# Sinkhorn normalisation moved onto 128 partitions as two chains, with half-size first loads and a new issue order

## The chip, the core and the metric

The kernel runs on one core of a Trainium2 chip. A core has five engines that run their own instruction streams: TensorE (PE in the profile; its weight loads are shown apart as PEld), VectorE (DVE), ScalarE (ACT), GpSimd (POOL) and SyncE (SP, which here only issues DMAs). They meet through semaphores. PSUM is the memory that TensorE writes and that DVE and ACT read; SBUF is the working memory.

The metric is the device time of one execution in microseconds, median of the runs. Before the change it is 155.96 us (three runs, 155.92 to 155.98).

## The reference

The computation is a block-sorted attention followed by a gated MLP, for 4 batches, 8 heads, 768 tokens, head size 64. Each head has an 8x8 matrix `sort_net`, normalised in five Sinkhorn rounds. Its result mixes the eight 96-token blocks of k and v, and each block of q attends only to its own mixed block.

```python
P = sort_net                                     # (4, 8, 8, 8)
for _ in range(5):
    P = np.exp(P - np.max(P, axis=-1, keepdims=True))
    P = P / (np.sum(P, axis=-1, keepdims=True) + 1e-09)
    P = P / (np.sum(P, axis=-2, keepdims=True) + 1e-09)
k_sorted = np.einsum('bhij,bhjcd->bhicd', P, k_b)      # v_sorted likewise
...                                              # per block: softmax(q k^T / 8) v
x = attn_out.transpose(0, 2, 1, 3).reshape(B, S, H * D)
h = np.maximum(x @ w_in, 0.0)                    # 512 -> 1024, halves u and v
v_n = (v - mu) / np.sqrt(var + 1e-06)
v_s = np.einsum('ts,bsd->btd', w_spatial, v_n) + b_spatial[None, :, None]
return (u * v_s) @ w_out
```

## The kernel before

The whole program is written as a list of short items, `ORDER`. Each item names a function (`u_KT`, `u_SC`, ...) and its arguments, and the items are issued in exactly that order; every engine takes its own instructions from the list in sequence. No scheduler changes it. The first argument of an item that uses TensorE is one of four PSUM buffers (0 to 3); an item that wants a buffer waits until the previous user's result has been copied out. The letter A or D says whether ACT or DVE makes that copy.

The items that matter here, with the engine work of each:

- `S0`, `SK:n`: load `sort_net` as 32 partitions (batch and head) by 64 values, then one Sinkhorn round n: an exponential on ACT, then six short DVE instructions (row sums, reciprocal, product, column sums, reciprocal, product; lines 238 to 249). Round 4 ends with a transpose on DVE (line 251).
- `MC`, `PR`: eight bf16 products that spread the normalised matrices over 128 partitions (line 256). `P0:lo:hi` multiplies them by a mask into `pd(0)`, the mixing matrices of batch 0, on DVE (line 270). `PC` copies the spread matrices to SBUF, and `PD:b:lo:hi` makes the mixing matrices of heads lo to hi of batch b from that copy on GpSimd (line 282).
- `L:what:b:lo:hi`: a load with cast from fp32 to bf16, issued on GpSimd's DMA queue (line 171 for q, k, v); `LH` loads half of q of batch 0 as fp32 on SP's queue and `QC` casts it on ACT. Loads rotate through eight buffers and eight semaphores.
- `KT`, `VT`: twelve products of two heads of k or v with `pd` (line 383) and one copy. `QT`, `QQ`: transposes of q (line 314). `VB`, or `VM` and `VC` (a copy and DMAs), bring mixed v into the layout that attention wants.
- `SC`: eight score products (line 442) and the exponential on ACT (line 447). `AT`: eight products with mixed v (line 488), a reciprocal and a product on DVE (lines 495, 496). `XT`, `XX` or `XD`: transposes of the attention output, on TensorE or by DMA.
- `VP`, `UP` (the two halves of the first linear layer, lines 554 and 597), `ST`, `LN`, `LA` (layer normalisation), `SP` (token mixing, line 609), `GT` (gate), `OP`, `OE`, `OS` (last layer, copy, store). The items from `SH` on are the end of the last batch, in smaller pieces.
- `DM:ps:n:w`: n products of zeros, w columns wide (line 226), whose results nobody reads.

The order around the change: DVE prepares constants, the five rounds `SK:0` to `SK:4` follow, with `DM` items and two `QT` items between them on TensorE; `PR`, four `P0` items and `PC` end the preparation, and the first `VT` and `KT` follow. The loads are issued in the order v, k, second half of q of batch 0, then v, q, k of batch 1, the weights, and so on.

An alternative path (`general_path`) repeats the computation with maxima subtracted. It is taken only when a check of the sums (`CK`, `CF`, `LF`) fires, which it does not with these inputs.

Of the kernel before, what the change touches and what calls it, by code (L numbers as in the profile page):

```python
# [21 lines left out]
KT:0:D:0:2 SC:2:0:0:1 VB:3:D:0:0 PD:1:4:8 KT:1:A:0:1 QT:0:D:0:2 IV:1 QT:2:A:0:3 VB:3:D:0:1 SC:0:0:1:0 VT:1:D:0:3  # L22
VT:2:A:0:2 L:wsa L:q:2:0:8 SC:3:0:0:0 PD:3:0:4 PD:3:4:8 BI AT:0:0:0:1 L:k:2:0:8 VB:1:D:0:3 SC:2:0:1:1 AT:3:0:0:0
VM:0:A:1:0 VB:1:D:0:2 SC:2:0:2:0 AT:3:0:1:0 SC:0:0:3:0 AT:1:0:2:0 SC:2:0:2:1 AT:3:0:1:1 VM:0:A:1:2 AT:2:0:3:0
XT:1:A:0:0:0 VM:0:D:1:3 QQ:3:D:1:2 SC:1:0:3:1 VM:2:D:1:1 XT:0:A:0:1:0 KT:1:A:1:2 L:q:3:0:8 AT:3:0:3:1 VC:1:4:8
KT:0:A:1:1 AT:2:0:2:1 KT:1:A:1:0 VC:1:0:4 QQ:3:D:1:0 KT:0:A:1:3 PD:2:0:4 XT:2:D:0:0:2 XT:1:D:0:1:2 PD:2:4:8 L:wo
SC:3:1:0:1 SC:0:1:2:0 VP:2:D:0:0:1 ST:0:0 SC:0:1:1:1 SC:1:1:3:1 ST:0:1 VP:3:A:0:4:5 VP:2:A:0:2 VP:1:A:0:3 ST:0:5
L:v:3:0:8 WW:2:A:4 ST:0:3 SC:3:1:3:0 AT:0:1:0:1 UP:1:A:0:1:0 ST:0:2 ST:0:4 AT:0:1:3:1 UP:2:A:0:0:0 LN:0:0:6 AT:3:1:2:0
# [37 lines left out]
def kernel(  # L66
# [123 lines left out]
    def load_sort_net():  # L190
        queue("S").dma_start(out=p_all, in_=sort_net.rearrange("b h i j -> (b h) i j"))
# [635 lines left out]
```

## Time and profile before

| | |
|---|---|
| median of three runs | 155.96 us |
| profiled execution, span from first to last instruction | 154.5 us (1.5 us less than the median of the runs) |
| PE busy, share of the span | 146.7 us, 95% |
| DVE busy | 115.4 us, 75% |
| ACT busy | 85.5 us, 55% |
| GpSimd busy | 39.4 us, 25% |
| mean granted TensorE clock | 0.999 of full speed |
| loads through GpSimd's queue | 12.19 MB, 48.8% of the time of the 16 DMA engines |

The profile is one execution, taken by the hardware profiler. Its views are read as follows. A group row gives line, engine, operation, output <- input and shape, number of instructions, busy time and mean duration in ns, then the idle time ahead of them and what ended it. A timeline row gives start, duration, engine, line, operation. A piece of the chain (start, duration, what) belongs to the one path that, followed back from the last instruction, released every next step. A row of windows gives a stretch, then busy time and number of instructions on PE, PEld, DVE, ACT and POOL, then granted clock, DMA share and GB/s. A busy PE is not a PE at its peak, since its instructions are pipelined.

### The profile page before, as it was taken

The page shows a single profiled execution, that of the slowest core. Times are in us where ns is not written, and L with a number is a line of the kernel's source. Part 1 is how long each engine was busy: PE and PEld are TensorE (multiplying, and loading weights), DVE is VectorE, ACT ScalarE, POOL GpSimd, SP SyncE. Part 2 cuts the span into 40 slices and gives each one's busy share as a digit, 9 for nine tenths or more (in the row PEclk, how much of TensorE's full clock was granted, in tenths as well). Part 3 has the DMA queues.
Part 4 walks back from the last instruction along what each step waited for, and adds up shares of the span by engine and source line. Part 5 has one row for each costly group of instructions (what it writes and reads, how often), then busy time and mean ns, then how long its engine had stood idle before and what let it go on. Part 6 is the DMA issues. An engine that isn't in the chain of part 4 may idle for free.

```text
span 154.5 us, 4033 instructions
## 1 busy us (share of the span) xinstructions
PE 146.7 (95%) x1689; PEld 95.7 (62%) x1689; DVE 115.4 (75%) x258; ACT 85.5 (55%) x116; POOL 39.4 (25%) x45
## 2 busy tenths in 40 slices
PE   6988988999999999999999999999999999999991
PEld 2436866764667777456777654656876556774760
DVE  3787889968899976299974886697977629855742
ACT  3345989787979245997777057357650072260040
POOL 7953663292020007000000044000000406103630
PEclk9999999999999999999999999999999999999999
DMA  2999999999999999990069358704708400307756
GB/s 68 270 204 203 204 206 204 209 216 248 223 205 256 205 231 245 208 195 15 4 118 125 67 102 167 182 3 37 205 0 215 163 0 4 132 4 284 268 191 220
DMA packets 30693, 24.36 MB, mean 158 GB/s; under 512 B 10384, under 2 KB 27792, under 8 KB 30672
## 3 DMA queue, kind: packets, MB, share of 16 engines
q0 software_dynamic: 14432, 12.19, 48.8%
q1 hardware_dynamic: 15664, 11.23, 28.8%
q10 hardware_dynamic: 576, 0.66, 1.2%
q8 instruction: 14, 0.23, 0.6%
q14 instruction: 7, 0.06, 0.1%
HBM read 24.78 MB, written 6.29 MB: 201 GB/s over the span
## 4 chain that ended last, share of the span: by engine, by line
PE 84%; DMA 7%; ACT 2%; DVE 2%; POOL 1%; issue 1%; POOLq 0%; ACTq 0%
PE ps L609 15%; PE ps L554 14%; PE ps L597 14%; PE ps L635 10%; DMA k_in<-in_k_dram 7%; PE ps L442 5%; PE ps L488 5%; PE ps L665 5%; PE ps L383 4%; PE ps L685 3%; PE ps L314 2%; PE ps L410 2%; PE ps L518 2%; ACT ex_all L447 2%; PE ps L531 1%; PE ps L401 1%
## 5 line engine op out<-in xcount | busy, mean ns | idle before, releaser
L626 POOL TENSOR_TENSOR gt<-z,u_sb 128x768 bf16<-128x768 f32 x7 | 11.4, 1640 | 77.0 <-DVE z L615 47.6
L447 ACT ACTIVATE ex_all<-ps 96x768 bf16<-96x768 f32 x32 | 24.7, 806 | 5.7 <-PE ps L442 5.5
L609 PE MATMUL ps<-wspT,v_sb 128*128 128x384 bf16 x144 | 25.1, 326 | 0.0
L597 PE MATMUL ps<-xT,w_in_sb 128*128 128x384 bf16 x128 | 22.8, 326 | 0.0
L496 DVE TENSOR_TENSOR x_sb<-ps,rec_all 96x512 bf16<-96x512 f32 x32 | 22.0, 686 | 1.1
L554 PE MATMUL ps<-w_in_sb,xT 128*128 128x512 bf16 x96 | 22.3, 380 | 0.0
L571 DVE BATCH_NORM_STATS2 stats<-v_sb 128x6 f32<-128x512 bf16 x24 | 16.3, 678 | 4.5 <-ACT v_sb L121 4.5
L115 ACT COPY o_sb<-ps 128x1024 f32<-128x1024 f32 (+1 forms) x12 | 10.9, 905 | 14.6 <-PE ps L685 9.1
L609 PEld LDWEIGHTS <-v_sb 128*128 128x128 bf16 x144 | 13.6, 97 | 8.6
L121 ACT ACTIVATE v_sb<-ps 128x1024 bf16<-128x1024 f32 (+1 forms) x11 | 10.3, 948 | 12.3 <-PE ps L554 12.3
L615 DVE TENSOR_TENSOR z<-ps,b_bc 128x768 f32<-128x768 f32 x12 | 11.4, 954 | 7.3 <-PE ps L609 4.6
L635 PE MATMUL ps<-w_out_sb,gt 128*128 128x256 bf16 x144 | 16.9, 273 | 0.0
L121 ACT ACTIVATE u_sb<-ps 128x768 bf16<-128x768 f32 x12 | 9.7, 811 | 12.7 <-PE ps L597 12.7
L597 PEld LDWEIGHTS <-w_in_sb 128*128 128x128 bf16 x128 | 11.8, 97 | 7.2
L635 PEld LDWEIGHTS <-gt 128*128 128x128 bf16 x144 | 13.8, 97 | 2.1
L554 PEld LDWEIGHTS <-xT 128*128 128x128 bf16 x96 | 8.7, 97 | 9.9
L488 PEld LDWEIGHTS <-ex_all 96*128 96x128 bf16 x256 | 10.7, 97 | 4.0 <-issue 0.5
L488 PE MATMUL ps<-vb,ex_all 96*128 96x65 bf16 x256 | 12.6, 193 | 0.5 <-ACT ex_all L447 0.5
L226 PE MATMUL ps<-warm 128*128 128x512 bf16 x36 | 9.5, 425 | 1.3 <-DVE warm L201 1.3
L442 PE MATMUL ps<-qT,kt_all 64*128 64x96 bf16 x256 | 9.8, 205 | 0.9 <-issue 0.4
L115 ACT CAST kt_all<-ps 128x768 bf16<-128x768 f32 x11 | 8.7, 801 | 2.2 <-PE ps L383 2.2
L442 PEld LDWEIGHTS <-kt_all 64*128 64x128 bf16 x256 | 6.4, 94 | 5.5 <-issue 3.3
(97 smaller groups left out, 202.6 us busy)
## 6 DMA issues: line engine op xcount, KB each, us to landing
out_dram<-o_sb SPq DMA_DIRECT2D x9, 512.0 KB, 4.6
v_in<-in_v_dram POOLq DMA_DIRECT2D x4, 768.0 KB, 21.4
k_in<-in_k_dram POOLq DMA_DIRECT2D x4, 768.0 KB, 23.7
vb<-vm SPq DMA_DIRECT2D x24, 99.0 KB, 5.8
q_in<-in_q_dram POOLq DMA_DIRECT2D x3, 768.0 KB, 28.2
ws_in<-in_moe_w_spatial_dram POOLq DMA_DIRECT2D x2, 576.0 KB, 26.6
w_in_sb<-in_moe_w_in_dram POOLq DMA_DIRECT2D x2, 512.0 KB, 24.9
q<-in_q_dram SPq DMA_DIRECT2D x1, 768.0 KB, 4.6
```

The source lines that it names most:

```text
L115: nc.scalar.copy(out=out, in_=in_)
L121: nc.scalar.activation(out=out, in_=in_, func=AF.Relu)
L442: nc.tensor.matmul(t[:, hh, 0:HW].rearrange("p (g x) -> p g x", g=G)[:, :, ii * TB:(ii + 1) * TB], lhsT=kT[rows, i * BLK:i * BLK + 128], r ...
L447: nc.scalar.activation(out=e_tile(b, hp, ih).rearrange("p h (x g) -> p h x g", g=G), in_=t[0:BLK, :, 0:HW].rearrange("p h (g x) -> p h x g ...
L488: nc.tensor.matmul(t[:, hh, ii * VW:ii * VW + D + 1], lhsT=e[:, c:c + 128], rhs=vb[b % 2][:, ih * NI + ii, 2 * hp + hh, 0:D + 1], start=Tr ...
L496: nc.vector.tensor_mul(out=x_sb[:, hp].rearrange("p i (h d) -> p h i d", h=2), in0=tv[:, :, :, 0:D], in1=_raw_ap(rec, 0, [rec.ap[0], [NI, ...
L554: nc.tensor.matmul(t[:, x, :], lhsT=st["xT", b][:, n // 3, kc, (n % 3) * 128:(n % 3 + 1) * 128], rhs=w_in_sb[:, kc, DH:DFF], start=(kc == ...
L571: nc.vector.bn_stats(out=stats, in_=st["v_sb", b, n])
L597: nc.tensor.matmul(t[:, x, 0:HW], lhsT=w_in_sb[:, kc, mc * 128:(mc + 1) * 128], rhs=st["xT", b][:, ih, kc, :], start=(kc == 0), stop=(kc = ...
L609: nc.tensor.matmul(t[:, x, 0:HW], lhsT=st["v_sb", b, n][:, mc * 128:(mc + 1) * 128], rhs=wspT[:, 3 * x:3 * x + 3, n, :], start=(n == 0), s ...
L615: nc.vector.tensor_add(out=z.rearrange("p (x c) -> p x c", x=2), in0=t[:, :, 0:HW], in1=b_bc.rearrange("p (x c) -> p x c", x=2),)
L635: nc.tensor.matmul(t[:, x, c:c + w], lhsT=st["gt", b, mc][:, (n0 + x) * 128:(n0 + x + 1) * 128], rhs=w_out_sb[:, mc, c:c + w], start=(mc = ...
```

## The change

`sort_net` is loaded as 128 partitions (head within half, column or row) by two halves of 16 heads, chain 0 for batches 0 and 1 and chain 1 for batches 2 and 3. `E0` does the first exponential and the row sums, `SX` and `SY` the first column sums, by an fp32 product with a matrix that marks which partitions belong to the same head. `SE` is a later round's exponential, with the column scale given to the activation as a per-partition factor, and the fp32 product that sums over a head's partitions; `SR` is its reciprocal, the product with it (with the sum along the free axis as a by-product), and the reciprocal of that sum. After the fourth `SR` the result is written as `p_end`, and `PR` needs a single bf16 product per chain. The DVE transpose is gone.

The masks that this needs (`MK`, `ML`, `MA`) are sums over an identity matrix, whose zeros are now written by DVE ahead of everything else; the small constants that DVE wrote are written by GpSimd (`CP`). The activation table load is an item, `TB`.

The first loads are k, v and q of batch 0 in halves: heads 0 to 3 of k, of v, then heads 4 to 7 of q, of k, of v. `P0` makes heads 0 to 3 only; heads 4 to 7 of batch 0 are made by `PD` on GpSimd, and `PC` is on ACT, once per chain. `VT` writes into its own padded buffers so that `VB` uses 128 columns of weights instead of 96. `VC` can take a range of heads and ACT's DMA queue.

All of `ORDER` is new. Among other things two pairs of `XT` items of batch 1 became `XX`, `QQ` of batch 1 became four `QT`, and ten of twelve whole `GT` items are on GpSimd instead of seven. The amount of work of the main products (`KT`, `VT`, `QT`, `SC`, `AT`, `VM`, `VP`, `UP`, `SP`, `OP`, `SH`, `OH`) is unchanged; the products of zeros fall from 36 of 512 columns to 15 of 512 and 5 of 256.

```diff
 ORDER = """
-S0 CO SK:0 BH LH:S:0 IV:2 L:v:0:0:8 SK:1 SK:2 ID MA L:k:0:0:8 L:q:0:4:8 DM:3:6:512 DM:0:6:512 L:v:1:0:8 L:q:1:0:8
-QC:A:0 SK:3 QC:A:1 MB SK:4 DM:2:6:512 DM:1:6:512 MC QT:2:D:0:1 DM:1:6:512 DM:3:6:512 PR:1 L:k:1:0:8 QT:2:A:0:0 P0:0:2
-L:wv L:wsb P0:4:6 P0:6:8 IV:0 P0:2:4 PC:D VT:0:A:0:0 KT:3:D:0:0 L:wu PD:1:0:4 VT:2:A:0:1 L:v:2:0:8 KT:1:A:0:3
...
+TB S0 LH:S:0 CO IV:0 ID L:k:0:0:4 MK L:v:0:0:4 MA ML L:q:0:4:8 E0 BH L:k:0:4:8 DM:2:4:512 SX:1:0 SX:0:1 SY:0
+DM:3:1:256 SY:1 CP SE:1:0:1 L:v:0:4:8 SR:0:1 L:v:1:0:8 DM:2:2:256 SE:0:1:1 DM:3:2:256 MC SE:1:0:2 SR:0:2 DM:2:3:512
+L:k:1:0:8 SR:1:1 SE:1:0:3 DM:3:2:512 MB QC:A:0 SE:0:1:2 SR:0:3 SR:1:2 DM:2:1:512 DM:3:1:512 SE:1:0:4 DM:2:2:512 SR:0:4
+SE:0:1:3 DM:3:2:512 PR:1:0 SR:1:3 QC:A:1 P0:0:2 P0:2:4 QT:3:D:0:0 PC:0:A PD:1:0:4 QT:2:D:0:1 L:q:1:0:8 KT:0:A:0:0
+KT:1:A:0:1 VT:3:D:0:0 SC:2:0:0:0 VT:0:D:0:1 SC:1:0:1:1 PD:0:6:8 PD:0:4:6 SC:3:0:1:0 VB:2:D:0:0 SC:0:0:0:1 L:wv
...
+KT:2:A:1:0 XT:3:D:0:1:2 QT:0:D:1:3 QT:1:D:1:1 PD:3:4:8 QT:3:D:1:0 SC:2:1:3:1 QT:0:D:1:2 VC:1:4:8 SC:1:1:1:1 SC:3:1:0:1 SC:2:1:0:0
+VP:0:A:0:5:1 VC:1:0:4:0:4 AT:1:1:1:1 VP:3:A:0:4 VP:2:A:0:2 IV:1 AT:1:1:3:1 VP:0:A:0:3 PD:2:0:4 SC:3:1:2:1 L:v:3:0:8
...
+    def u_E0():
...
+        nc.scalar.activation(out=p_all, in_=p_all, func=AF.Exp)
+        nc.vector.reduce_sum(out=first[:, 0:2], in_=p_all, axis=AX.X)
+        nc.vector.reciprocal(out=row, in_=plus(first[:, 0:2]))
+    def u_SX(ps, c):
+        c = int(c)
+        nc.vector.scalar_tensor_tensor(
+            out=p_row[c], in0=_raw_ap(p_all, c * NB, [p_all.ap[0], [0, NH], [1, NB]]),
+            scalar=row[:, c:c + 1], in1=same_head, op0=ALU.mult, op1=ALU.mult)
+        nc.tensor.matmul(
+            sums(c, ps), lhsT=p_row[c].rearrange("p h j -> p (h j)"), rhs=of_block, start=True, stop=True)
+    def u_SY(c):
+        c = int(c)
+        nc.vector.reduce_sum(out=first[:, 2 + c:3 + c], in_=sums(c), axis=AX.X)
+        nc.vector.reciprocal(out=col[:, c, 0:1], in_=plus(first[:, 2 + c:3 + c]))
+    def u_SE(ps, c, n):
+        c, n = int(c), int(n)
+        e = p_exp[c][n - 1]
+        nc.scalar.activation(
+            out=e, in_=sums(c) if n == 1 else p_one[c][n - 2], func=AF.Exp, scale=col[:, c, n - 1:n])
+        nc.tensor.matmul(
+            sums(c, ps), lhsT=same_head.rearrange("p h j -> p (h j)"), rhs=e, start=True, stop=True)
+    def u_SR(c, n):
+        c, n = int(c), int(n)
+        e, one, total, rec = p_exp[c][n - 1], p_one[c][n - 1], p_sum[:, c, n:n + 1], p_rec[:, c, n - 1]
+        nc.vector.reciprocal(out=rec, in_=sums(c))
+        nc.vector.scalar_tensor_tensor(
+            out=one, in0=e, scalar=1.0, in1=rec, op0=ALU.mult, op1=ALU.mult, accum_out=total)
+        nc.vector.reciprocal(out=col[:, c, n:n + 1], in_=plus(total))
         if n == 4:
-            nc.vector.transpose(out=p_t, in_=p16)
...
+            nc.vector.scalar_tensor_tensor(
+                out=p_end[:, c], in0=_raw_ap(one, 0, [one.ap[0], [1, NB], [0, NH]]),
+                scalar=col[:, c, n:n + 1], in1=_raw_ap(of_head, 0, [of_head.ap[0], [0, NB], [1, NH]]),
+                op0=ALU.mult, op1=ALU.mult)
+    def u_PR(ps, c):
+        c = int(c)
+        pr = ps_tile(ps)[:, 0, 0:NB * NH]
+        nc.tensor.matmul(
+            pr, lhsT=spread.rearrange("p j t -> p (j t)"), rhs=p_end[:, c].rearrange("p i h -> p (i h)"),
+            start=True, stop=True)
+        st["pr", c] = pr
...
-            nc.tensor.transpose(t[:, i, :], vT[:, i * BLK:(i + 1) * BLK], ident)
+            nc.tensor.transpose(t[:, i, :], vT[:, i * BLK:i * BLK + 128], ident)
```

More of the change, by code (lines that the diff above doesn't have):

```diff
@@ L24 @@
[L24 to L28, printed above, removed]
@@ L216, in u_MC @@
     def u_MC():
-        nc.scalar.copy(out=spread, in_=ident[0:BH, 0:BH].to_broadcast([BH, BH, TB]))
+        nc.scalar.copy(out=spread, in_=of_block.to_broadcast([128, NB, TB]))
     def u_IV(n):
@@ L253, in u_PR, with plus @@
[L253 to L260 removed]
+    def plus(x):
+        if "general" in st:
+            nc.vector.tensor_scalar_add(out=x, in0=x, scalar1=1e-9)
+        return x
```

188 lines of the change are left out of this document (100 added, 88 removed).

## The prediction

> **What bounds the kernel now.** I read the page first, then the chain of waits in order of time, then the timeline of the first 14 us and windows over the stage behind it. On the page TensorE (PE) is nearly always busy:
>
> ```profile
> span 154.5 us, 4033 instructions
> PE 146.7 (95%) x1689; PEld 95.7 (62%) x1689; DVE 115.4 (75%) x258; ACT 85.5 (55%) x116; POOL 39.4 (25%) x45
> ```
>
> The chain says where that is the path (start, length, what):
>
> ```profile
> 2.88 10.96 DMA k_in<-in_k_dram
> 13.89 0.88 PE ps L383 x24
> ...
> 27.90 0.82 ACT ex_all L447
> 28.75 0.53 PE ps L383 x12
> ...
> 30.89 0.67 PE ps L314 x24
> ...
> 32.68 0.45 PE ps L442 x16
> 33.13 1.83 PE ps L554 x8
> ...
> 73.43 1.75 PE ps L635 x16
> ...
> 75.75 1.30 PE ps L597 x8
> ...
> 79.40 0.21 DVE rec_all L495
> 79.64 0.70 DVE x_sb L496
> ...
> 83.72 1.95 PE ps L609 x12
> ```
>
> Three stretches are seen. Until 13.89 PE waits for the load of k. Until 28.75 copies on ACT and DVE alternate with PE. From there PE runs without a break to the end, but for 1 us at 79.4. So what the change does ahead of 33.13, the first `VP`, moves the end one for one, while its edits behind that count only if they stop PE.
>
> How the first stretch is made, from the timeline:
>
> ```profile
> 2.43 0.26 ACT L238 ACTIVATE p_all<-p_all 32x64 f32<-32x64 f32 x1 [0.32 <-DMA p_all<-in_sort_net_dram]
> 2.64 0.29 POOL masks.py:199 TENSOR_SCALAR_AFFINE_SELECT ident<-ident 128x128 bf16<-128x128 bf16 x1
> 4.19 0.26 ACT L238 ACTIVATE p_all<-p_all 32x64 f32<-32x64 f32 x1 [1.51 <-DVE p_all L249]
> 11.90 0.36 PE L256 MATMUL ps<-p_t,spread 32*128 32x32 bf16 x8
> 12.30 1.41 DVE L270 TENSOR_TENSOR pd<-mask,ps 128x256 bf16<-128x256 bf16 x4 [0.39 <-PE ps L256]
> 13.89 0.53 PE L383 MATMUL ps<-pd,k_in 128*64 128x128 bf16 x12 [0.59 <-DMA k_in<-in_k_dram]
> ```
>
> A Sinkhorn round takes 1.76 us (2.43 to 4.19). The rounds, the transpose and `PR` (11.90) end in `P0`, which starts at 12.30, the point that I measure from. Then k is late by another 0.59.
>
> **The new front.** Prices of one instruction, from the groups by form:
>
> ```profile
> L577 ACT ACTIVATE rstd<-mv,eps 128x6 f32<-128x6 f32 x4 | 1.2, 296 | 3.0 <-DVE mv L572 3.0
> L242 DVE RECIPROCAL rowsum<-rowsum 32x8 f32<-32x8 f32 x4 | 0.8, 191 | 0.1
> L249 DVE TENSOR_TENSOR p_all<-p_all,colsum 32x64 f32<-32x64 f32 x4 | 0.8, 212 | 0.1
> L711 DVE TENSOR_REDUCE ends<-first 32x1 f32<-32x8 f32 x3 | 0.4, 139 | 0.0
> L211 DVE TENSOR_REDUCE m<-ident 128x16 f32<-128x128 bf16 x1 | 0.4, 365 | 0.0
> L725 PE MATMUL ps<-bad,ones 128*1 128x5 bf16 x1 | 0.2, 166 | 0.0
> L597 PEld LDWEIGHTS <-w_in_sb 128*128 128x128 bf16 x128 | 11.8, 97 | 7.2
> ```
>
> No fp32 product stands in this trace; its price x is the unknown of this front. Low end: the small bf16 product, 0.17. [...]
>
> [...]
>
> The way to the first `P0`: the identity is ready at about 1.4 (DVE's zeros at about 1, then the select, 0.29, which comes at 2.64 today). Four DVE instructions on masks, three at 0.365 and a copy of 128x128 fp32 at about 0.28 (between 0.212 for 64 columns in L249 and 0.35 for 256 in `P0`, 1.41 / 4), end at 2.9, later than the first exponential (2.69), so DVE is the gate. `E0`: 0.14 + 0.19, to 3.25. `SX`: 0.28 + x, to 4.0. `SY`: 0.14 + 0.14 and the gaps, to 4.4. A round of a chain: exponential with a per-partition factor 0.30 (L577, which also reads one), x, reciprocal 0.19, product 0.21, reciprocal of one column 0.14, five handovers of 0.03: 1.45 in place of 1.76. Four rounds end at 10.2, `p_end` (0.28) at 10.5. DVE then has the third `SR` of chain 1 ahead of `P0`, 0.6, under which `PR` lies. `P0` at 11.1 instead of 12.30: **-1.2 us**. [...]
>
> Chain 1's rounds lie in chain 0's pauses: DVE needs 0.54 for each `SR`, and 0.30 + x are free. The two `QC` casts are in ACT's order between exponentials, where ACT idles 1.51 a round now. The zeros that moved to GpSimd lie behind four load issues and are read much later. They cost nothing while those covers last; a late `QC` would hold one exponential, at most 0.8.
>
> **The first loads.** Bytes moved in each stretch, last column in GB/s:
>
> ```profile
> 0.00:4.00 4.00, 2.71 (x7) 1.04 (x8) 1.60 (x11) 1.54 (x2) 3.03 (x10) 1.00 0.32 79
> 4.00:8.00 4.00, 3.98 (x19) 1.56 (x16) 2.99 (x14) 1.52 (x5) 4.00 (x6) 1.00 1.23 261
> 12.00:16.00 4.00, 3.13 (x89) 2.67 (x89) 3.25 (x7) 2.71 (x4) 1.86 (x2) 1.00 1.31 203
> ```
>
> q (0.79 MB) and the first half of k (0.39 MB) make 1.18 MB: 0.32 come by 4.0, 0.86 more at 261 GB/s by 7.3. The first half of v is there by about 9. Both are ahead of `P0`, so the wait of 0.59 goes: **-0.6**, counted inside the next stage. The second halves come at about 14 and 16, behind the work on the first.
>
> **The stage to the first `VP`.** Today it is 33.13 - 12.30 = 20.8 us. In the window from 12 to 16 DVE is busy 3.25 and ACT 2.71 of 4, and in the chain (27.90) it is such work that PE waits for, so I count the work of these engines, not PE's.
>
> ```profile
> L447 ACT ACTIVATE ex_all<-ps 96x768 bf16<-96x768 f32 x32 | 24.7, 806 | 5.7 <-PE ps L442 5.5
> L282 POOL TENSOR_TENSOR pd<-mask,prep_sb 128x512 bf16<-128x512 bf16 x6 | 6.5, 1095 | 3.3 <-DVE prep_sb L117 3.0 <-PE ps L383 0.3
> L171 POOL DMA_DIRECT2D q_in<-in_q_dram x4 | 3.5, 863 | 4.5 <-PE ps L488 2.5 <-PE ps L383 1.9
> L115 ACT CAST kt_all<-ps 128x768 bf16<-128x768 f32 x11 | 8.7, 801 | 2.2 <-PE ps L383 2.2
> L117 DVE COPY qT<-ps 128x1536 bf16<-128x1536 bf16 x3 | 2.8, 948 | 0.2 <-PE ps L314 0.2
> L117 DVE COPY qT<-ps 128x768 bf16<-128x768 bf16 x2 | 1.1, 532 | 0.1
> ```
>
> DVE: two `P0` (0.7), `PC` (about 0.4), two `QQ` (1.9) and one `XT` of `QT`'s size (0.5) leave, 3.5; six `QT` (3.2) and the last `SR` of chain 1 with its `p_end` (0.8) come, 4.0; one `VM` leaves for one `VT`. DVE gets 0.5 more. ACT is now the fuller one: it has to reach the copy of `KT:2:A:1:0`, whose buffer the scores `SC:2:1:3:1` take, with 15 copies at 0.80, 8 exponentials at 0.806, two `PC` at some 0.35 and one `SE`, 19.4 us. Then PE has four score groups (0.45 for two, the x16 at 32.68) and a q group (half of 0.67, the x24 at 30.89) to go, 1.2. That is 20.6; for waits that busy sums leave out I add 0.6 (between 0 and 1.3): 21.2 against 20.8, **+0.4**, with the k wait gone from it. Behind it PE has less left: two score groups (0.45) are already done, against the small products of chain 1 and one bf16 product, 0.05 to 0.5: **-0.4** at the low end, 0 at the other.
>
> One wait is new: heads 4 to 7 of batch 0 come from GpSimd, behind `PC` (0.35), a `PD` of 512 columns (1.1) and a load issue (0.9), as two halves of 0.55 each, at 14.6. The `KT` that reads them has two `KT` copies and three exponentials (4.0) ahead of it on ACT, to about 16, and SP, PE and DVE have no one queued behind GpSimd there; without that cover it would cost at most the 0.6 that a later `PD` half takes.
>
> Nothing else is on the path: `VB` with wider weights, `XX` for `XT`, the gates on GpSimd and `VC` on ACT's queue lie in stages where PE never waits today. What they cost without that cover is the range's business: 1 us either way, as large as the one stop at 79.4.
>
> Sum: -1.2 + 0.4 - 0.4 = -1.2 us on a span of 154.5, so 153.3. The median of runs is 1.5 above the span: **154.8 us**.
>
> **Rivals.** *Quick products (A).* x is 0.17: five times 0.29 less, 153.3 us. For it: weights of the mark matrices never change in `SE`. Against: 97 ns a load in every row.
>
> *ACT becomes the bound (B), slower.* ACT's items from `P0` to the first `VP` sum to 22.7 (the 19.4 and four exponentials that `VP` does not need) against 19.3 today (14 copies, 10 exponentials). If `VP` has to wait for them through the PSUM buffers, the stage is 22.7 + 0.6 = 23.3, not 21.2: 156.9. It decides from 1.2 us of that wait on. Against: `VP:0` uses a buffer that DVE frees.
>
> *Slow products (C), slower.* From x = 0.70 the front's gain is gone (0.24 x 5); at 0.90 the time is 157.0. [...]
>
> *The gain is given back behind (D), no change.* The transposed q of batch 3 comes by DMA, and SP takes its items in order:
>
> ```profile
> 77.68 3.74 SPq L370 DMA_TRANSPOSE qT<-qp  x1
> 94.32 0.59 SPq L650 DMA_DIRECT2D out_dram<-o_sb  x1
> 106.13 1.48 SPq L506 DMA_TRANSPOSE xT<-x_sb  x1
> qT<-qp SPq DMA_TRANSPOSE x1, 7.6
> ```
>
> Now `QX` comes ahead of the `XD` items. In the new order `XD:2:1`, which waits for `AT:0:2:0:0`, and a store stand ahead of it on SP: 0.9 for that `AT`'s DVE work, 1.5, 0.6 and 7.6 to landing, 10.6 us. Over these PE has, to the first scores of batch 3, two `OP` (1.75), a `UP` (1.30), an `SP` (1.95), one `VP` tile (0.9), four `KT` (half of 0.88 each), 9.4, and a few groups of `AT` and `VM`. There is hardly a margin: with these DMAs 1.2 later than PE the time is 156.0.
>
> **How the numbers follow.** Forecast 0.46 (154.8, its own range 154.0 to 155.5), A 0.15, B 0.13, C 0.14, D 0.12. Faster or slower means by over 0.2% (0.31 us), about what a measurement of this kernel tells from no change: faster 0.61 (forecast and A), same 0.12 (D), slower 0.27 (B and C). The range 153.3 to 157.0 leaves out half of C and half of A: less than 2 in 10.
>
> **What would show it.** The first `P0` at 11.1 (A: 9.7, C: over 12.3); rounds of 1.45; x as the length of the fp32 products; no idle of PE before the first `KT` for k; the first `VP` at 32.3 with no ACT exponential as its releaser (B); no DMA ahead of the first scores of batch 3 (D). The prediction is wrong if PE stops more than 1 us in all after its first `VP`, or if the end moves without the first `P0` having moved.

## The result, and the profile after

The change makes the kernel slower: 160.68 us (median of four runs, 160.11 to 161.19) against 155.97 beside them, a ratio of 1.0297 with a 95% interval of 1.028 to 1.0315 (further ratios below, all to the kernel before, have theirs in brackets). The forecast was 154.8, faster; its range, 153.3 to 157.0, does not hold the time. In some executions of the changed kernel's variants the granted clock of TensorE falls to 0.50 for 3.4 to 6.8 us (kernels 8 and 3), and these are up to some 2% longer (163.50 us against 159.78 in kernel 3); the ratios leave out only the longest of these, and the ratio of kernel 1 still holds two (160.03 and 160.27 us).

| | before | after |
|---|---|---|
| span of the profiled execution | 154.5 us | 158.1 us (its run 160.58) |
| first `P0` starts | 12.30 | 12.92 |
| first `KT` starts | 13.89 | 13.53 |
| first `VP` starts | 33.13 | 34.42 |
| TensorE's last product ends | 151.11 | 154.72 |
| TensorE idle between the last two | 0.30 | 3.81 |

The head of the page after, and the row of 40 slices for PE:

```profile
span 158.1 us, 4079 instructions
PE 148.2 (94%) x1687; PEld 98.2 (62%) x1687; DVE 115.1 (73%) x269; ACT 84.0 (53%) x122; POOL 47.0 (30%) x56
PE   5999999996999999999899999599999999999991
```

TensorE is as busy as before, and two of the slices, the tenth and the twenty-sixth, have holes that the text below finds. Windows of the trace after, chosen around those holes (window, its length, then busy time and instructions of each engine, granted clock, share of DMA, GB/s):

```profile
36.00:40.00 4.00, 2.40 (x22) 1.18 (x21) 0.89 (x2) 2.48 (x4) 0.37 (x2) 1.00 1.27 223
78.00:79.00 1.00, 0.57 (x13) 0.30 (x6) 1.00 (x2) 1.00 (x3) 0.00 (x0) 1.00 0.00 0
99.00:102.00 3.00, 1.24 (x21) 0.92 (x20) 2.56 (x4) 0.00 (x0) 0.99 (x1) 1.00 0.71 111
102.00:154.72 52.72, 52.70 (x405) 33.51 (x403) 38.31 (x87) 18.10 (x26) 13.93 (x11) 1.00 0.35 113
```

Length less PE's busy time is the idle: 1.60, 0.43 and 1.76. These three stops are all but 0.02 of the 3.81, since in the stretches between them PE is busy throughout. The same reckoning for the kernel before gives 0.03, 0.25 and 0.02:

```profile
33.13:79.00 45.87, 45.84 (x547) 29.95 (x547) 36.87 (x76) 33.26 (x45) 6.84 (x7) 1.00 1.00 180
79.00:84.00 5.00, 4.75 (x87) 3.87 (x85) 2.57 (x5) 4.63 (x6) 0.00 (x0) 1.00 1.35 186
84.00:151.11 67.11, 67.09 (x562) 42.25 (x559) 49.08 (x104) 25.39 (x34) 13.32 (x10) 1.00 0.44 119
```

The chain of waits says what lies ahead of each:

```profile
32.21 7.23 DMA vb<-vm
...
75.23 0.83 DVE qp L120
...
77.86 0.70 DVE x_sb L554
...
78.60 1.47 PE ps L655 x8
...
94.61 0.84 ACTq L481
...
95.48 6.15 DMA vb<-vm
```

The first stop ends with a GpSimd memset (L248), `IV:1`, which writes the ones columns of the second `vb`. In the new order it stands behind `VC:1`, whose DMAs write the same buffer, ones columns included; so it waits for the last of them, and `AT:1:1:3:1` waits for it. The timeline there:

```profile
36.16 0.41 PE L546 MATMUL ps<-vb,ex_all 96*128 96x65 bf16 x8
39.63 0.21 POOL L248 MEMSET vb<- 96x128 bf16 x1 [8.64 <-DMA vb<-vm]
39.89 0.40 PE L546 MATMUL ps<-vb,ex_all 96*128 96x65 bf16 x8 [1.60 <-POOL vb L248]
```

At 36.16 an `AT` already reads that buffer, so the data that the next `AT` wants had landed. The second stop ends with DVE, which has all four copies of `QP` to make: the letter P in `QP:P:3:2` means DVE as well, since the copy helper knows only ACT and DVE. The third ends with `VC:3`, issued at 92.3 to 95.5, when the last mix of v was copied, and landed at 101.6.

The front after, from the timeline (chain 0's exponentials, one round's fp32 product, dummies, the end):

```profile
4.65 0.27 ACT L291 ACTIVATE p_exp<-ps,col 128x8 f32<-128x8 f32 x1 [1.87 <-DVE col L286]
4.97 0.60 PE L293 MATMUL ps<-p_exp,same_head 128*128 128x8 f32 x2
6.34 0.30 ACT L291 ACTIVATE p_exp<-p_one,col 128x8 f32<-128x8 f32 x1 [0.81 <-DVE col L302]
8.05 0.30 ACT L291 ACTIVATE p_exp<-p_one,col 128x8 f32<-128x8 f32 x1 [1.41 <-DVE col L302]
9.75 0.30 ACT L291 ACTIVATE p_exp<-p_one,col 128x8 f32<-128x8 f32 x1 [0.48 <-DVE col L302]
9.94 1.01 PE L253 MATMUL ps<-warm 128*128 128x512 bf16 x2
11.94 0.35 DVE L304 SCALAR_TENSOR_TENSOR p_end<-p_one,col,of_head 128x128 bf16<-128x128 f32 x1
12.13 0.65 PE L253 MATMUL ps<-warm 128*128 128x512 bf16 x2
12.62 0.22 PE L312 MATMUL ps<-p_end,spread 128*128 128x128 bf16 x1
12.92 0.73 DVE L325 TENSOR_TENSOR pd<-mask,ps 128x256 bf16<-128x256 bf16 x2
13.53 1.05 PE L441 MATMUL ps<-pd,k_in 128*64 128x128 bf16 x24
```

Rounds take 1.70, not 1.45, and two dummies at 9.94 take 1.01 where two at 12.13 take 0.65: until some 12 us TensorE runs them at half speed. In the kernel before, the twelve at 9.20 take 2.77 in all, 0.23 each.

Not all of the loss is in the span. The four runs lie 2.39 to 2.48 above their spans. The kernel before, in the runs that were taken beside the experiments, lies 1.74 to 1.94 above its own, and spans of 154.5 belong to runs of about 156.3. So a run of before at the median has a span near 154.15; of the 4.7 us some 4.1 are in the span and 0.6 outside it.

### The profile page after: what moved, and what is told of

It reads as the page before. It is cut to its first block, busy times and chain, and to the rows that moved or that the text cites. A ratio compares the mean times of both kernels' runs of the same rounds, so it can differ in the third digit from the quotient of the medians.

```text
span 158.1 us, 4079 instructions
## 1 busy us (share of the span) xinstructions
PE 148.2 (94%) x1687; PEld 98.2 (62%) x1687; DVE 115.1 (73%) x269; ACT 84.0 (53%) x122; POOL 47.0 (30%) x56
## 3 DMA queue, kind: packets, MB, share of 16 engines
q10 hardware_dynamic: 1744, 1.99, 4.1%
## 4 chain that ended last, share of the span: by engine, by line
PE 70%; DMA 10%; ACT 8%; DVE 6%; SPq 3%; issue 1%; ACTq 1%; POOL 0%; POOLq 0%
PE ps L655 13%; PE ps L667 11%; PE ps L693 10%; PE ps L612 9%; DMA vb<-vm 8%; PE ps L723 5%; ACT ex_all L505 4%; PE ps L546 4%; PE ps L253 3%; PE ps L743 3%; SPq L481 3%; PE ps L441 2%; PE ps L500 2%; PE ps L293 2%; DVE x_sb L554 2%; PE ps L372 1%
## 5 line engine op out<-in xcount | busy, mean ns | idle before, releaser
L684 POOL TENSOR_TENSOR gt<-z,u_sb 128x768 bf16<-128x768 f32 x10 | 16.3, 1650 | 68.1 <-DVE z L673 42.9
L505 ACT ACTIVATE ex_all<-ps 96x768 bf16<-96x768 f32 x32 | 24.2, 805 | 10.4 <-PE ps L500 10.1
L612 PE MATMUL ps<-w_in_sb,xT 128*128 128x512 bf16 x96 | 23.4, 379 | 0.0
L124 ACT ACTIVATE v_sb<-ps 128x512 bf16<-128x512 f32 (+1 forms) x15 | 10.7, 712 | 23.2 <-PE ps L612 22.9
L118 ACT COPY o_sb<-ps 128x1024 f32<-128x1024 f32 (+1 forms) x10 | 8.8, 882 | 15.7 <-PE ps L743 10.5
L553 DVE RECIPROCAL rec_all<-ps 96x8 f32<-96x8 f32 x32 | 6.4, 199 | 10.8 <-PE ps L546 10.5
L124 ACT ACTIVATE u_sb<-ps 128x768 bf16<-128x768 f32 x13 | 10.5, 811 | 5.0 <-PE ps L655 4.7
L736 POOL TENSOR_TENSOR gt<-z,u_sb 128x512 bf16<-128x512 f32 (+1 forms) x5 | 5.2, 1057 | 15.8 <-DVE z L729 15.7
L253 PE MATMUL ps<-warm 128*128 128x512 bf16 (+1 forms) x20 | 8.6, 540 | 1.4 <-DVE warm L216 1.4
L339 POOL TENSOR_TENSOR pd<-mask,prep_sb 128x512 bf16<-128x512 bf16 (+1 forms) x8 | 7.9, 989 | 6.6 <-ACT prep_sb L118 6.5
## 6 DMA issues: line engine op xcount, KB each, us to landing
k_in<-in_k_dram POOLq DMA_DIRECT2D x3, 768.0 KB, 25.5
```

The lines of the kernel that those rows point to most:

```text
L124: nc.scalar.activation(out=out, in_=in_, func=AF.Relu)
L253: nc.tensor.matmul(t[:, 0, 0:int(w)], lhsT=warm[:, 0:128], rhs=warm[:, 0:int(w)], start=True, stop=True)
L505: nc.scalar.activation(out=e_tile(b, hp, ih).rearrange("p h (x g) -> p h x g", g=G), in_=t[0:BLK, :, 0:HW].rearrange("p h (g x) -> p h x g ...
L612: nc.tensor.matmul(t[:, x, :], lhsT=st["xT", b][:, n // 3, kc, (n % 3) * 128:(n % 3 + 1) * 128], rhs=w_in_sb[:, kc, DH:DFF], start=(kc == ...
L684: eng.tensor_mul(out=gt, in0=st["z", b, mc], in1=u)
```

## The experiments

Kernels 1 to 4 have one line less ahead of the functions, so their line numbers are lower by one than in the changed kernel.

**1. The memset early.**

```diff
-... VP:2:A:0:2 IV:1 AT:1:1:3:1 ...
+... L:k:1:0:8 IV:1 SR:1:1 ...
```

> The changed kernel, with the zeroing-free memset `IV:1` (the ones columns of the second `vb`) back among the first GpSimd items, ahead of every write of batch 1 into that buffer. Theory: the stop of TensorE at 38.3 to 39.9 is only this memset, which in the new order stands behind `VC:1` and so waits for the last of its transfers (8.6 us on GpSimd); the transfer that `AT:1:1:3:1` itself reads has landed before 36. Then that idle of 1.6 goes whole and the time is 160.7 - 1.6 = 159.1 (158.8 to 159.4). Rival: the transfers of `VC:1` are late themselves; then TensorE's idle there keeps DMA vb<-vm as its releaser and at most the 0.45 from landing to product goes: 160.2 or more. The two later stops stay as they are in both.

Ratio 1.0217 (1.0151 to 1.0282), four runs from 157.50 to 160.27; the profiled run is the quickest, 157.50 us, its span 155.3. The idle between 33 and 40 is 0.06:

```profile
33.00:40.00 7.00, 6.94 (x92) 3.83 (x87) 3.49 (x9) 6.00 (x9) 4.08 (x5) 1.00 1.24 231
```

So the memset was the whole first stop. The profiled run is below the 158.8 that was expected at the least, for two more reasons that its trace shows: the third stop is 1.02 here instead of 1.76, and the first `P0` comes at 12.71 instead of 12.92.

**2. The last mix of v, and `VC:3`, earlier.**

```diff
-... AT:0:2:1:0 VM:3:D:3:3 ... VC:3:4:8:0:4 ... VC:3:0:4:0:4:A ...
+... VP:3:A:2:4 VM:3:D:3:3 VC:3:4:8:0:4 VC:3:0:4:0:4 KT:1:A:3:0 ...
```

> The changed kernel, with `VM:3:D:3:3` and all of `VC:3` moved ahead of the four `KT` of batch 3, and both halves of `VC:3` on SP. Theory: the stop of 1.76 at 99.9 to 101.7 comes from the last mix of v, which ends on DVE at 92.1, so that `VC:3` is issued at 92.3 to 95.5 and lands at 101.6. Issued some 3.5 us earlier it lands before the products that read it: idle gone, 160.7 - 1.7 = 159.0 (158.7 to 159.4). Rival: the landing hangs on what else moves then (the transposes on SP, `XD:2:0`), so an earlier issue gains nothing or SP's later transposes become the wait: 160.3 or more.

Median 159.42 us, ratio 1.0226 (1.019 to 1.0261), profiled run 159.01; the theory said 158.7 to 159.4. A window and TensorE's timeline:

```profile
95.00:103.00 8.00, 8.00 (x80) 4.63 (x78) 6.16 (x11) 2.26 (x3) 1.58 (x1) 1.00 0.49 59
```

```profile
86.93 0.48 PE L467 MATMUL ps<-v_in,pd 128*128 128x384 bf16 x2 [0.69 <-ACT v_sb L123]
```

The third stop is gone. A new one of 0.69 comes with the edit: the mix waits for a PSUM buffer that ACT has yet to empty.

**3. `QP` on ACT.**

```diff
-... QP:D:3:1 ... QP:P:3:2 ... QP:P:3:3
+... QP:A:3:1 ... QP:A:3:2 ... QP:A:3:3
```

> The changed kernel, with three of the four copies `QP` of batch 3 on ACT, as they were before; in the new order all four run on DVE (the letter P in them means DVE too). Theory: between 71.2 and 78.6 the chain runs through DVE, and TensorE's wait of 0.43 at 78.6 is what these copies (0.6 to 0.9 each, three of them in this stretch) leave over: the wait goes, 160.7 - 0.4 = 160.3, and nothing else moves, since the next stop is set by an order on TensorE and the queues. Rival: this backlog of DVE also makes the stop at 101.7 (vm's last copy is DVE's): then more than 1 us goes.

Ratio 1.0268 (1.0211 to 1.0325), its two quickest runs 159.78 and 159.81. In its profiled execution the third stop is 2.67 long and the granted clock is 0.50 from 101.2 to 108.0, so its trace cannot be compared with that of the changed kernel. The interval of the times overlaps that of the changed kernel, and the spans of the two quickest runs, 157.9, are only 0.3 below its mean span: by itself this run decides nothing about 0.4 us. Kernels 5 and 9 carry the edit on.

**4. No dummies between the rounds.**

```diff
-DM:3:1:256 ... DM:2:2:256 ... DM:3:2:256 ... DM:2:3:512 ... DM:3:2:512 ... DM:2:1:512 DM:3:1:512 ... DM:2:2:512 ... DM:3:2:512
```

> The changed kernel without the 16 dummy products of zeros that stand between the fp32 products; the first four at 1.35 stay. Theory 1 (the dummies are on the path of the rounds): the fourth product of chain 0 no longer waits 0.4 to 0.7 for them, nor `PR` 0.3, and the first `P0` comes at 11.9 to 12.2 instead of 12.92. Theory 2 (TensorE runs at half speed until it has been kept busy, as the 0.43 of a 512-wide dummy here and its 0.23 from 4 us on in the kernel before suggest): without them the first products behind `P0` take twice as long for about 3 us, which gives back 0.9 to 1.5. Time by 1 alone 159.8, by both 160.2 to 161.2. Where neither holds `P0` stays at 12.9 and the time at 160.7.

Ratio 1.0393 (1.0312 to 1.0475), profiled run 161.23: slower still, though the first `P0` comes 0.66 earlier, at 12.26. The first `KT` group:

```profile
13.27 1.49 PE L440 MATMUL ps<-pd,k_in 128*64 128x128 bf16 x24
```

The same 24 products took 1.05 in the changed kernel. Both effects are seen: the dummies stand on the path of the last round and of `PR`, and without them TensorE starts the real work at a lower speed (the 24 products of `QT` ahead of this group take 1.49 too, against 0.86 in the changed kernel). The sizes were missed, since `P0` comes just behind the 11.9 to 12.2 of theory 1 and all four runs are above 161.2; the third stop is also longer here, 2.3. The rounds still take 1.70, so in the first three the dummies cost nothing.

**5. The three stops mended together.**

```diff
 IV:1 as in 1, QP as in 3, and
-... UP:0:A:2:1:1 OS:0:4 QX:3:0:4 AT:2:2:2:0 ... VM:3:D:3:3 ... VC:3:4:8:0:4 ... VC:3:0:4:0:4:A
+... UP:0:A:2:1:1 VM:2:D:3:3 OS:0:4 QX:3:0:4 VC:3:4:8:0:4 VC:3:0:4:0:4 AT:1:2:2:0 ...
```

> The changed kernel with the three stops mended together: the memset `IV:1` early; `VM:3:D:3:3` with all of `VC:3` ahead, this time in a PSUM buffer (2) that is free, since in buffer 3 the mix waited 0.7 for ACT; three `QP` on ACT. Theory: the three idles (1.6, 1.76, 0.43) and nothing else make the loss behind the first `P0`, and they add: 160.7 - 3.8 = 156.9, with a clock that rises earlier or later in the front 156.2 to 157.3. It does not reach the time before, because TensorE has 1.0 more to do behind the first `KT` and 0.4 to 1.0 lie outside the span. Rival: a stop that is taken away comes back at the next late transfer or buffer: 158.0 or more, with idles of TensorE over 1 us in all between 34 and 105.

157.15 us, ratio 1.0078 (1.0061 to 1.0096): the stops add up as forecast. Two smaller ones are left, both made by the edits: 0.92 at 84 to 86 (buffer 1, behind DVE) and 0.36 at 65 (a `QP` on ACT).

**6. The same with light dummies at the end of the front.**

```diff
-DM:2:1:512 DM:3:1:512 ... DM:2:2:512 ... DM:3:2:512 ... PR:1:0
+DM:2:1:128 DM:3:1:128 ... DM:2:2:128 ... DM:3:2:128 ... PR:1:0
```

> The kernel of the run before, with the last dummies of the front (seven of 512 columns, between the third `SR` of chain 0 and `PR:1:0`) cut to 128 columns. Theory 1, the dummies lie on the path: the fourth product of chain 0 and `PR` come 0.6 to 0.9 earlier and the time is that much below the run before. Theory 2, TensorE's speed depends on how long it has been busy: with less work in these 3 us the step to full speed, seen at 10.6 to 12.4 with all dummies and at 16.7 with none, comes after 13.5, and products behind `P0` run at half speed: the time is 0.3 to 1.0 above the run before, although `P0` is earlier. The first `KT` group of 24 tells them apart: 1.05 at full speed, 1.5 or more below it.

157.77, ratio 1.011 (1.0082 to 1.0138): 0.6 above kernel 5, theory 2 (the dummies cut are six, not seven). `P0` comes at 12.53 instead of 12.74, but the first `KT` group takes 1.49.

**7. The halves of k and v alone, in the kernel before.**

```diff
-... L:v:0:0:8 SK:1 SK:2 ID MA L:k:0:0:8 L:q:0:4:8 ...
+... L:k:0:0:4 SK:1 SK:2 ID MA L:v:0:0:4 L:q:0:4:8 L:k:0:4:8 L:v:0:4:8 ...
```

> The kernel before, with one part of the change alone: the first k and v loaded in halves, in the order k, v, q, k, v. Theory: the wait of 0.59 of the first `KT` for k goes and nothing is late in its place, as in the changed kernel: 156.0 - 0.6 = 155.4. Rival: v's first half or k's second half is late for the products behind (`VT:0:A:0:0`, `KT:1:A:0:3`), and the 0.6 is only moved: 155.9 to 156.2.

155.87 us, ratio 0.999 (0.998 to 1.0001), ten runs: 0.1 of the 0.6 us by the median, but the runs lie apart, four at 155.39 to 155.60 and six at 155.79 to 156.09. The profiled one is the quickest, 155.39, and has the whole gain: the wait of the first `KT` is gone (it starts at 13.07), and the first `VP` starts at 32.18 instead of 33.13. Two smaller waits are left in it. The second `VT` comes at 13.73, when the fourth `P0` ends, 0.33 later than the spacing of the groups ahead of it, and TensorE waits for the k of batch 1:

```profile
27.80 0.53 PE L383 MATMUL ps<-pd,k_in 128*64 128x128 bf16 x12 [0.26 <-DMA k_in<-in_k_dram]
```

What holds back the other six runs is not shown.

**8 and 10. The new front with the old order behind it, twice.** Kernel 8 puts the front of the changed kernel ahead of the old order; kernel 10 mends its place for `P0` and lays chain 1's last step further back.

```diff
+(front as after) ... QC:A:1 QT:3:D:0:1 QT:2:A:0:0 P0:0:2 ... QT:0:D:0:2 SE:1:1:4 SR:1:4 ... PR:1:1 PC:1:A VT:1:D:0:3 ...   (8)
+(front as after) ... P0:0:2 P0:2:4 QT:2:A:0:0 QT:3:D:0:1 ... AT:3:0:0:0 SE:1:1:4 SR:1:4 ... PR:1:1 PC:1:A PD:3:0:4 PD:3:4:8 AT:1:0:2:0 ...   (10)
```

> The changed kernel's front (both Sinkhorn chains, halves of k and v, its dummies) up to the fourth exponential, and behind it the order of the kernel before, with chain 1's last step and its copy in the ACT-bound stretch. Theory: the loss lies in the order of the work behind the front and not in the new Sinkhorn steps; the first `KT` comes at 13.2 to 13.6 instead of 13.89, no stop over 0.4 follows, and the time is 155.4 to 156.2 (0.3 to 0.7 less, up to 0.5 more outside the span). Rival: chain 1's 0.4 + 0.2 on TensorE, its DVE and ACT steps and the later rise of the clock cost more than the front gains: 156.5 or more even with the old order.

> The new front with the old order behind it, laid out anew: in the run of that kind before, a q copy stood on DVE ahead of `P0`, which came at 13.79, so that it did not tell the two theories apart. Now `P0:0:2` and `P0:2:4` stand as in the changed kernel, and chain 1's last step lies further back, at the first `AT`. Theory: the loss is the order's; first `P0` at 12.6 to 13.0, first `KT` at 13.1 to 13.6, time 155.5 to 156.6. Rival: chain 1's last step, its copies on ACT and the half speed before 11 to 12 cost more than the front gains, so the new steps lose with the old order too: 157.0 or more.

Ratios 1.0244 (1.0218 to 1.027) and 1.0212 (1.0183 to 1.0242). These are the rivals' times, some 3 us above what the theories said, but neither run tells order and steps apart. In 8, `P0` came only at 13.79, behind a copy on DVE, and the granted clock is 0.50 from 22.1 to 25.5. In 10, `P0` came at 12.84, but chain 1's last step stops TensorE where it was put, 0.71 for its exponential and 0.96 for `PC`; and after these stops the profiled execution shows a granted clock of 0.50:

```profile
22.88 0.39 PE L293 MATMUL ps<-p_exp,same_head 128*128 128x8 f32 x2 [0.71 <-ACT p_exp L291]
...
26.20 0.40 PE L546 MATMUL ps<-vb,ex_all 96*128 96x65 bf16 x8 [0.96 <-ACT prep_sb L118]
```

```profile
25.00:28.40 3.40, 2.16 (x47) 1.68 (x44) 2.47 (x7) 2.57 (x5) 0.40 (x1) 1.00 1.28 205
28.50:31.80 3.30, 3.30 (x39) 2.00 (x37) 2.61 (x4) 1.32 (x2) 2.83 (x3) 0.50 1.19 210
```

What they do show is that chain 1's last step stops TensorE where these two orders put it. Whether the new steps would pay in the old order stays open.

**9. No stop left.** Kernel 5 with its own two idles taken away.

```diff
-... UP:0:A:2:1:1 VM:2:D:3:3 ... AT:1:2:2:0 VP:3:A:2:4 KT:1:A:3:0 LA:1:3 KT:0:D:3:3 ... QP:A:3:1
+... UP:0:A:2:1:1 AT:1:2:2:0 VM:2:D:3:3 ... VP:3:A:2:4 LA:1:3 KT:0:D:3:3 KT:1:A:3:0 ... QP:D:3:1
```

> The kernel with the three stops mended, and its two new idles taken away too: 0.92 at 84 to 86, where the first `KT` of batch 3 waits for the buffer of an `AT` whose DVE work lies behind the copy of vm (now `AT:1:2:2:0` stands ahead of `VM:2:D:3:3`, and `KT:0:D:3:3` ahead of `KT:1:A:3:0`), and 0.36 at 65 behind a `QP` on ACT (now DVE's again, as in the changed kernel). Theory: the idles are the price, so the time is 157.15 - 0.9 - 0.36 = 155.9 (155.5 to 156.4), within 0.3% of the kernel before. Rival: what is left is more than idle (TensorE's extra work and half-speed products in the front), and a mended stop comes back elsewhere: 156.7 or more.

156.40 us in twelve runs (155.93 to 156.73), ratio 1.0019 (1.0006 to 1.0032): at the upper end of what was forecast, and still not below the kernel before. All waits of PE in its trace:

```profile
PE ps L253 <- DVE warm L216: 1.4, 1, 1.4
PE ps L280 <- DVE p_row L277: 0.5, 1, 0.5
PE ps L500 <- DVE vm L120: 0.3, 1, 0.3
PE ps L546 <- ACT ex_all L505: 0.2, 1, 0.2
```

From the first `KT` to its last product TensorE takes 151.22 - 13.97 = 137.25 us here; in the kernel before it is 151.11 - 13.89 = 137.22. So in these two executions the new order, without its stops, is worth what the old one was, the first `P0` comes no earlier (13.37 in this execution), and the runs lie 1.99 to 2.14 above their spans.

**11. The kernel before without its dummies.**

```diff
-DM:3:6:512 DM:0:6:512 ... DM:2:6:512 DM:1:6:512 ... DM:1:6:512 DM:3:6:512
```

> The kernel before without its 36 dummy products. There no Sinkhorn step runs on TensorE, so the dummies stand on nobody's path. Theory (TensorE's speed depends on its being busy for some microseconds): the first `P0` stays at 12.2 to 12.4, but TensorE steps up only after 3 us or more of real work, at 15 to 19; the first `KT` and `VT` groups take near twice the 0.53, and the time is 156.8 to 158.0. Rival: the dummies only fill, and the time stays at 155.8 to 156.2.

156.69 us, ratio 1.0049 (1.003 to 1.0067): a little less than forecast, because the first `P0` comes earlier, not at the same time:

```profile
11.81 1.41 DVE L270 TENSOR_TENSOR pd<-mask,ps 128x256 bf16<-128x256 bf16 x4
...
12.44 0.90 PE L383 MATMUL ps<-pd,v_in 128*64 128x128 bf16 x12
13.64 0.85 PE L383 MATMUL ps<-pd,k_in 128*64 128x128 bf16 x12 [0.30 <-DMA k_in<-in_k_dram]
```

So the dummies held `PR` by 0.5 in the kernel before too. Their worth is the speed: without them groups of twelve take 0.85 to 0.90 instead of 0.53.

**12 and 13. More dummies first.** Kernel 9 with eight, and with sixteen, ahead of the first fp32 product.

```diff
-DM:2:4:512
+DM:2:8:512   (12)
+DM:2:16:512   (13)
```

> The kernel with no stop left behind the front, with eight dummies in place of four ahead of the first fp32 product (DM:2:8:512). Theory (in the front the rounds run at TensorE's half speed, since its first four dummies are too short to bring the step up, and the dummies between the rounds pace them): eight dummies last to 4.4 to 4.8 and delay the first product from 3.6 by up to 1.2; where the step comes with them, rounds shrink from 1.70 to 1.4 or less, the last waits behind dummies halve, and the first `P0` comes at 11.8 to 12.3, the time at 155.0 to 155.8; where the step is still missed (it has come at 4.05 to 4.81 in the kernel before, after 2.8 to 3.5 of dummies), `P0` is 1 us later and the time 157.0 to 157.6, so single runs should fall into two groups. Rival: the rounds are bounded by ACT, DVE and the handovers; then `P0` is at 13.5 or later in all runs and the time at 157.0 or more.

> The same with sixteen dummies first, which last to 6.5 or more and so bring the step up in any case, at the price of a first product some 3 us late: a measurement of the rounds at full speed. Theory: rounds of 1.35 to 1.50 (1.45 was forecast), the two halves of an fp32 product some 0.3 from start to end in place of 0.60, from the first product `SX` to `P0` 7.0 to 8.0 us in place of 9.3. Rival: the rounds stay at 1.65 or more and the stretch at 9 or more, since the fp32 weight loads or the other engines set them, or since TensorE falls back to half speed between the products.

Twelve: 157.28, ratio 1.007 (1.0052 to 1.0088), six runs from 156.68 to 157.58, no two groups, none near 155.8; in its trace `P0` comes at 14.06, and two dummies at 11.99 still take 1.01. Eight are not enough in that trace. The median alone fits both the branch without the step (157.0 to 157.6) and the rival (157.0 or more). Thirteen, one run (159.28), is the measurement that tells them apart. ACT's timeline (chain 0 are 8.47, 9.95, 11.45 and 13.15), TensorE's, and two windows:

```profile
8.47 0.53 ACT L291 ACTIVATE p_exp<-ps,col 128x8 f32<-128x8 f32 x2 [5.61 <-DVE col L286]
...
9.95 0.30 ACT L291 ACTIVATE p_exp<-p_one,col 128x8 f32<-128x8 f32 x1 [0.76 <-DVE col L302]
11.45 0.30 ACT L291 ACTIVATE p_exp<-p_one,col 128x8 f32<-128x8 f32 x1 [1.20 <-DVE col L302]
...
13.15 0.30 ACT L291 ACTIVATE p_exp<-p_one,col 128x8 f32<-128x8 f32 x1 [0.48 <-DVE col L302]
```

```profile
8.79 0.39 PE L293 MATMUL ps<-p_exp,same_head 128*128 128x8 f32 x2 [0.41 <-ACT p_exp L291]
...
11.80 0.60 PE L293 MATMUL ps<-p_exp,same_head 128*128 128x8 f32 x2
```

```profile
7.40:10.70 3.30, 2.36 (x19) 1.67 (x18) 1.11 (x8) 1.02 (x4) 0.47 (x2) 1.00 1.31 203
10.70:14.10 3.40, 3.40 (x11) 1.72 (x10) 2.04 (x17) 1.52 (x4) 0.00 (x0) 0.51 1.31 202
```

At full speed a round is 1.48 and 1.50, and an fp32 product 0.39: the forecast of 1.45 was nearly right for that speed. But the speed does not last: after 3.3 us with 2.36 of work the granted clock is 0.51, the product takes 0.60, and the next round is 1.70 again. The 0.20 to 0.22 between the rounds matches the 0.21 between the products. From the first product (7.75) to `P0` (16.07) it is 8.3, between the 7 to 8 of the theory and the 9.3 before.

**14. What the front can give without the new steps.**

```diff
 halves as in 7, and
-... DM:3:6:512 PR:1 ... P0:0:2 ... P0:4:6 P0:6:8 IV:0 P0:2:4 ... KT:1:A:0:3 ... KT:1:A:0:1
+... DM:3:3:512 PR:1 ... P0:0:2 ... P0:2:4 P0:4:6 IV:0 P0:6:8 ... KT:1:A:0:1 ... KT:1:A:0:3
```

> The kernel before with the halves of k and v, two more edits that the runs point to: `KT` of heads 2 and 3 ahead of that of heads 6 and 7 (in the run with halves alone, `KT:1:A:0:3` waited 0.3 for k's second half), with `P0:2:4` second; and nine dummies instead of twelve ahead of `PR` (in the kernel before without dummies the first `P0` came at 11.81 instead of 12.30, so the last dummies hold `PR` by 0.4 there). Theory: both waits lie on the path to the first `VP` and TensorE keeps its full speed: first `P0` at 11.8 to 12.0, time 156.0 - 0.4 - 0.5 = 155.1 (154.9 to 155.5), faster than both kernels. Rival: the stretch behind `P0` is set by the copies on ACT and DVE or by k's second half, which come no earlier: 155.7 to 156.0.

155.47 us, ratio 0.9967 (0.9955 to 0.9979): faster than both kernels, at the upper end of what was expected. The expectation misread one thing: the 0.3 that kernel 7 waited for k was not `KT:1:A:0:3` but the first `KT` of batch 1, at 27.8, and that is where this kernel loses part of what it gains:

```profile
12.03 1.41 DVE L270 TENSOR_TENSOR pd<-mask,ps 128x256 bf16<-128x256 bf16 x4
```

```profile
27.83 0.53 PE L383 MATMUL ps<-pd,k_in 128*64 128x128 bf16 x12 [0.61 <-DMA k_in<-in_k_dram]
```

That group started at 28.75 before. The load lands at 27.8 in kernels 7 and 14 alike, so with these loads an earlier front is worth 0.9 at most up to there. From there on the traces of the two kernels run alike, and their profiled runs take the same time (155.39 and 155.41). What kernel 14 has over kernel 7 is that all of its six runs lie there (155.37 to 155.62), and not four of ten.

## Why the prediction was wrong, point by point

The terms of the sum, in the profiled executions (stops: TensorE's idle behind the first `VP`; work: its time from there to its last product, less that idle):

| | forecast | measured |
|---|---|---|
| first `P0` | -1.2 | +0.62 (12.30 to 12.92) |
| from there to the first `VP` | +0.4 (21.2) | +0.67 (20.83 to 21.50) |
| TensorE's work behind it | -0.4 to 0 | -1.19 (117.68 to 116.49) |
| stops behind it | 0 | +3.51 (0.30 to 3.81) |
| sum, of the span | -1.2 | +3.6 (+4.1 between median runs) |
| outside the span | 0 | about +0.6 |

*The step that failed* is the sentence "Nothing else is on the path: `VB` with wider weights, `XX` for `XT`, the gates on GpSimd and `VC` on ACT's queue lie in stages where PE never waits today." A stage of before says nothing about a stage whose order is new. The three stops are mended by edits of a few items each, and together they bring 160.68 to 156.40 (kernels 1, 2, 5 and 9), some 0.4 of it outside the span. The memset `IV:1` was given no price, although it had moved behind the DMAs that write its buffer; nor were the `QP` copies, three of which had gone from ACT to DVE; and `VC:3` was named, without asking when its source would be ready. The bound for all of it, "1 us either way", came from one stop of the old order, and that was misread: the chain runs 1 us through DVE at 79.4, but TensorE's idle there is 0.25. The price of a wait for a late DMA could have been read from the median of 5.8 us that these transfers took to land in the kernel before.

*The front.* "`P0` at 11.1 instead of 12.30" was missed by 1.82. The first exponential of the loop comes 0.25 late; three rounds of 1.70 instead of 1.45 make 0.75; the fourth, with two half-speed dummies ahead of its product, takes 2.19 up to `p_end` and makes 0.74; the rest, with dummies ahead of `PR`, 0.08. The price 1.45 is nearly right at full speed (1.48 and 1.50 in kernel 13). What failed is the speed. The 1.45 holds 0.46 for x, the length of an fp32 product, a term that no run shows: what the runs showed in its place is 0.39 at full speed (kernel 13) and 0.60 at half. The forecast gave x as one number, though in the trace of the kernel before the dummies of the first 3 us are 0.43 apart and later ones 0.21 to 0.23. The granted clock's column stands at 1.00 ahead of that step as well as behind it. The small products of the rounds take 0.39 to 0.60 each on the path and did not bring the speed up by themselves (kernel 4, where the first `KT` group still takes 1.49), so their place on this engine and the dummies that it needs are in each other's way: fewer dummies make `P0` earlier and the products behind it slower (kernels 4 and 6), more of them first make it later (12).

*k's wait* went, as forecast: nothing waits for k ahead of 13.53. By itself in the old order that is worth 0.1 in the median, not 0.6 (kernel 7); four of its ten runs have most or all of the 0.6, and what the others lack is not shown.

*The stage to the first `VP`*, counted by ACT's and DVE's work, was right to 0.3 in its length, but the reason given is not shown. From the first `KT` to the first `VP`, before and after:

```profile
13.89:33.13 19.24, 17.86 (x421) 14.55 (x422) 16.96 (x31) 16.54 (x23) 10.51 (x13) 1.00 1.28 206
13.53:34.42 20.89, 20.08 (x459) 15.81 (x454) 18.64 (x39) 18.69 (x28) 11.75 (x15) 1.00 1.27 221
```

TensorE has 2.2 more to do here and idles 0.81 instead of 1.38, while ACT, which was counted as the fuller engine, has 18.69 of 20.89. Over half of TensorE's 2.2 is work that stood behind the first `VP` before, so that the two middle terms of the table belong together; that the length came out is in part luck. Rival B, by which ACT's whole 22.7 would be on the path, gave 23.3, and did not happen.

*Rivals.* C named the right engine, but put the loss in x alone, and by its 0.70 the measured 0.60 for a product still gave a gain. The half speed came ahead of `P0`, in the dummies too (1.01 for two, as late as 11.04); behind `P0` the first `KT` group of 24 takes 1.05. D looked for a late transfer in the wrong place: no DMA stands ahead of the scores of batch 3, while two `vb<-vm` stand ahead of `AT`. Of the two tests that would show the prediction wrong, the first came out: TensorE stops 3.81 behind its first `VP`. The second did not as it is worded, since the first `P0` did move, by 0.62, though the end moved by 3.6.

*The 1.5 between span and median* was wrong too; by the later runs it is about 1.8 for that kernel, its profiled execution being longer than the median one. For the changed kernel it is 2.4, and 1.9 to 2.6 for its variants. One edit moves it: kernel 3, with three copies moved from DVE to ACT, has 1.9. Nothing in a trace explains that, and the cause stays open.

## What to carry to other kernels

When a list of work is reordered by hand or by a planner, look in the new order at every instruction whose place against a transfer has changed (a memset behind a DMA into the same buffer, a copy that feeds a transfer) and at which engine each copy is on; that an engine never waited in the old order proves nothing. Before a latency chain is put on TensorE, ask at what speed TensorE will be there, and read it from the lengths of equal products; here the clock's column stood at 1.00 while they took twice as long (dummies 0.43 apart, later 0.21 to 0.23). A gain at the front has to be followed to the next fixed time, here the landing of a load, before it is counted.

## What the runs showed that was not expected

TensorE's granted clock fell with no pause over 1 us ahead of it: in kernel 13 after a stretch of 3.3 us with 2.36 of work, in which the longest idle is 0.53, and in kernel 10 after 3.4 us with 2.16 and a longest idle of 0.96. Behind that it stands at 0.50 for some 3.4 us in both, and as long in kernel 8 (22.1 to 25.5). The busy time alone does not decide it: stretches as long hold less work in the changed kernel (1.80 in the 3.40 us up to 39.89, with one pause of 1.60) and in kernel 4 (1.52 in the 3.40 us up to 102.00), and the clock is at 1.00 behind both. What decides it stays open. Nor does the step up come at one time: two dummies at 10.95 take 0.59 in kernel 1, and two at 11.04 take 1.01 in the changed kernel, behind the same items on TensorE. And in the changed kernel TensorE counts as busy for 3.88 of the 4 us from 4 to 8, yet the two dummies at 9.94 still run at half speed (1.01, against 0.65 at 12.13). Whether the size of the products has a part in that was not tried by itself.
